# Another order for the ending of a convolution, GELU and rational-function kernel

## The chip, the cores and the metric

The kernel runs on one core of one Trainium2 chip. The metric is device time in microseconds of one execution, the median of several runs.

## The reference, cut to what matters

```python
# x: (2, 4096, 192); weight: (8, 7); w_in: (192, 2048); w_out: (2048, 192), two of each
w = softmax(weight)                       # per head, over the 7 taps
x = causal_depthwise_conv(x, w)           # 24 channels to a head
h = x.reshape(8192, 192) @ w_in1
g = h * sigmoid(1.702 * h)
x2 = g @ w_out1
h = x2 @ w_in2
P = a[0] + a[1] * h + a[2] * h**2 + a[3] * h**3
Q = 1 + abs(b[0]) * abs(h) + abs(b[1]) * h**2
out = (P / (Q + 1e-6)) @ w_out2           # (8192, 192)
```

## The kernel before, in words

The 8192 tokens are worked in 16 tiles of 512 (`NB = 16`, tiles 0 to 15). The 2048 hidden features are 16 blocks of 128, taken in 8 units of two blocks (`NS = 8`). The code writes the order of all engines by hand; each engine runs its own instructions in the order in which the program issues them.

For a tile n, the first layer is `h_product(0, n, i)` for unit i, then GELU on ACT, a split of the result into two float16 halves (`g1_high` on POOL, `g1_low` on DVE, into tiles `hl`), and the first output product `o1_main` and `o1_side`, which sums x2 of the whole tile in one PSUM tile `po` of the pool `ps_o`. x2 is scaled by a power of two: `x2_red` (DVE, maximum over the columns), `all_max` (a small TensorE product that spreads it over the partitions), `scales` (DVE), and `x2_split`, which writes x2's upper half (`high`, ACT) and lower half (`low`, DVE).

The second layer is `h_product(1, n, i)` ("product i" below; it needs both halves of x2), 24 matmuls into one PSUM tile `ph`. `unit` reads it: an absolute value and a linear step on ACT (L535, L536), two numerator steps on DVE (L537, L538). `denominator` (DVE, L543) makes Q; `log` and `inverse` (ACT, Ln and Sigmoid, L549 and L553, each kind in need of its own function table) turn it into 1/Q; `quotient` (DVE, L557) makes P/Q. `o2_chunk(n, i, k)` is the second output product of one block, 8 matmuls (L446) into another tile `po`; a pair of chunks (k = 0, 1) belongs to a unit.

PSUM has a pool `ps_h` of three buffers of two banks, for the `ph` tiles and small ones, and `ps_o` of one buffer of two banks.

The tiles overlap: the front phase of step j makes the first layer of tile j + 1 and the second layer of tile j; the back phase makes the first output product of tile j + 1, the logarithms and inverses of tile j, and the x2 scaling of tile j + 1. Output chunks of tile j that aren't done yet stand in a list `late_pe` and are issued between the products of the next step. `late_step` issues the quotients of units 4 to 7 of the tile before.

In the last step there is no later tile. The back phase then copies x2 from PSUM to SBUF (ACT, L691) before the scaling, since `po` of `ps_o` is needed for the output of tile 14. Four chunks of tile 14 are issued in the back phase, the other twelve in `last_phase`, which makes the products of tile 15 and its quotients, stores tile 14, and does all chunks of tile 15 at the end. The rows and names use the running numbers of the code: tile 14 is `NB - 2` and tile 15 is `NB - 1`.

Of the kernel before, what the change touches and what calls it, by code (L numbers as in the profile page):

```python
# [8 lines left out]
F32 = mybir.dt.float32  # L9
F16 = mybir.dt.float16  # L10
# [5 lines left out]
P = 128  # L16
# [4 lines left out]
def kernel(  # L21
# [30 lines left out]
    p2 = ctx.enter_context(tc.tile_pool(name="p2", bufs=2))  # L52
    p1 = ctx.enter_context(tc.tile_pool(name="p1", bufs=1))
    tiny = ctx.enter_context(tc.tile_pool(name="tiny", bufs=3))
    ps_h = ctx.enter_context(tc.tile_pool(name="ps_h", bufs=3, space=bass.MemoryType.PSUM))
    ps_o = ctx.enter_context(tc.tile_pool(name="ps_o", bufs=1, space=bass.MemoryType.PSUM))

    stack = ExitStack()
    stage = stack.enter_context(tc.tile_pool(name="stage", bufs=2))
    rings = []  # L60
# [11 lines left out]
    cst = const.tile([P, 8], F32, name="cst")  # L72

    def ps_tile(name):
        return ps_h.tile([P, 2, 512], F32, tag="h", name=name)

    def pow2_of(dst, src):
        nc.vector.tensor_scalar(out=dst, in0=src, scalar1=1e-30, scalar2=None, op0=ALU.max)
# [4 lines left out]
    def all_max(red, pm):  # L83

        nc.tensor.matmul(out=pm[:, 0, 0:P], lhsT=red.to_broadcast([P, P]), rhs=ident, start=True, stop=True)  # L85
# [217 lines left out]
    def flat_of(t):  # L303
        return t.rearrange("p k t -> p (k t)")[:, 0:W]
# [108 lines left out]
    def h_product(m, n, i, between=None):  # L413
        ph = ps_tile("ph")
        at = (ph, m, n, i)
        if m:
            h_side(*at, start=True)
            h_main(*at, stop=True)
        else:
            h_main(*at, start=True)  # L420
            if between is not None:
                between()
            h_side(*at, stop=True)
        return ph
# [53 lines left out]
    def o2_chunk(n, i, k, groups=range(NG)):  # L478
        pp = units_t[n][i][0]
        o_chunk(1, n, NS * k + i, ((pp, k, wo2[:, NS * k + i]),), groups)  # L480
# [47 lines left out]
    def unit(n, ph, pp=None):  # L528

        sc = sc2_t[n]  # L530
        if pp is None:
            pp = rings[0].tile([P, 2 * T], F32, tag="p", name="pp")
        qq = rings[0].tile([P, 2 * T], F32, tag="q", name="qq")
        h = ph.rearrange("p k t -> p (k t)")
        nc.scalar.activation(out=qq, in_=h, func=ACTF.Abs, scale=sc[:, 2:3])  # L535
        nc.scalar.activation(out=pp, in_=h, func=ACTF.Identity, scale=sc[:, 7:8], bias=sc[:, 6:7])  # L536
        nc.vector.tensor_tensor(out=pp, in0=pp, in1=h, op=ALU.mult)  # L537
        nc.vector.scalar_tensor_tensor(out=pp, in0=pp, scalar=sc[:, 5:6], in1=h, op0=ALU.add, op1=ALU.mult)  # L538
        units_t.setdefault(n, []).append((pp, qq))

    def denominator(n, i):
        qq = units_t[n][i][1]
        nc.vector.scalar_tensor_tensor(  # L543
            out=qq, in0=qq, scalar=ab[:, 14:15], in1=qq, op0=ALU.add, op1=ALU.mult
        )
# [5 lines left out]
    def inverse(n, i):  # L551
        qq = units_t[n][i][1]
        nc.scalar.activation(out=qq, in_=qq, func=ACTF.Sigmoid, scale=-1.0)  # L553

    def quotient(n, i):
        pp, qq = units_t[n][i]
        nc.vector.scalar_tensor_tensor(  # L557
            out=pp, in0=pp, scalar=ab[:, 0:1], in1=qq, op0=ALU.add, op1=ALU.mult
        )

    def each(f, n, steps):
        for i in steps:
            f(n, i)

    def late_step(n, i):

        if i < NS // 2:
            quotient(n, NS // 2 + i)
# [4 lines left out]
    def store(n):  # L573
        t = p1.tile([P, NG, D], F32, tag="on", name="on")
        for k in range(2):
            nc.scalar.activation(
                out=t[:, 2 * k:2 * k + 2], in_=out_tile(n, k), func=ACTF.Copy
            )
        po_t.pop((1, n)), sc2_t.pop(n)
        nc.sync.dma_start(out=out[n * T:(n + 1) * T].rearrange("(g p) d -> p g d", p=P), in_=t)  # L580
# [3 lines left out]
    def store_half(n, k):  # L584

        if k == 0:
            on_t[n] = p1.tile([P, NG, D], F32, tag="on", name="on")
        t = on_t[n][:, 2 * k:2 * k + 2]
        if k:
            nc.vector.tensor_copy(out=t, in_=out_tile(n, k))  # L590
        else:
            nc.scalar.activation(out=t, in_=out_tile(n, k), func=ACTF.Copy)
        rows = out[n * T + k * 2 * P:n * T + (k + 1) * 2 * P]
        nc.sync.dma_start(out=rows.rearrange("(g p) d -> p g d", p=P), in_=t)

    late_pe, early, second = [], {}, {}

    def last_phase(j):

        def units(i, late=0):  # L600
            pp = hl_tile().rearrange("p two t -> p (two t)").bitcast(F32)
            unit(j, h_product(1, j, i), pp)
            late_step(j - 1, i)
            for _ in range(late):
                late_pe.pop(0)()
            denominator(j, i)

        def own(i, groups=range(NG)):
            for k in range(2):
                o2_chunk(j, i, k, groups)  # L610

        first = NS // 2
        for i, late in enumerate((0, 0, 2, 1, 2, 2)):
            units(i, late)
        each(log, j, range(first))
        units(first + 2, 1)
        each(inverse, j, range(first))
        each(quotient, j, range(first - 1))
        units(first + 3, len(late_pe))
        quotient(j, first - 1)  # L620
        po_t[1, j] = ps_tile("po")
        for i in range(first):
            own(i)
        store(j - 1)
        each(log, j, range(first, NS))
        for i in range(first, NS):
            inverse(j, i)
            quotient(j, i)
        for i in range(first, NS - 1):
            own(i)  # L630
        for groups in (range(0, 2), range(2, 4)):
            own(NS - 1, groups)
        store_half(j, 0)
        store_half(j, 1)

    def front_phase(j, n1, extras):

# [30 lines left out]
    def back_phase(j, n1, n2, conv, splits):  # L668

        if conv is not None:  # L670
            x_transpose(conv)
            for k in range(K):
                x_conv_pool(conv, k)
        for part in (o1_main, o1_side):
            for i in range(NS):
                o1_product(part, n1, i, splits[i])
                if part is o1_main:
                    log(j, i)
            if part is o1_main and conv is not None:
                x_max(conv)  # L680
                x_scales(conv)
                x_scale_out(conv)
        chunks = [lambda i=i, k=k: o2_chunk(j, i, k) for i in range(NS) for k in range(2)]
        each(inverse, j, (0, 1, 2, 3))
        quotient(j, 0)
        src = po_t.pop((0, n1))
        pm = ps_tile("pm2")
        sc = sc2_t[n1] = tiny.tile([P, 24], F32, tag="sc2", name="sc2")
        if n2 is None:
            copy = p1.tile([P, 2, T], F32, tag="xc", name="copy")  # L690
            nc.scalar.activation(out=flat_of(copy), in_=flat_of(src), func=ACTF.Copy)  # L691
            src = copy
        red = x2_red(src)
        if n2 is None:
            chunks.pop(0)()
            all_max(red, pm)
        else:
            early[n2, 0] = h_product(0, n2, 0, lambda: all_max(red, pm))
            early[n2, 1] = h_product(0, n2, 1)
        scales(pm, sc)  # L700
        x2_split(n1, src, sc, sc1_t.pop(n1)[:, 6:7])
        each(quotient, j, (1, 2, 3))
        each(inverse, j, (4, 5, 6, 7))
        if n2 is not None:
            second[n1, 0] = h_product(1, n1, 0)
        for f in chunks[:3]:
            f()
        late_pe.extend(chunks[3:])
# [138 lines left out]
    with tc.manual_schedule():  # L847
        for j in range(NB - 1):
            n1, n2, conv = (j + d if j + d < NB else None for d in (1, 2, 3))
            extras = {i: [] for i in range(NS)}  # L850
            if conv is not None:
                x_load(conv)
                extras[2].append(lambda: x_red(conv))
            if j == 0:
                xc_t[2] = ps_o.tile([P, 2, 512], F32, tag="o", name="pc")
                for m in range(2 * K):
                    extras[m // 3].append(lambda m=m: x_conv_matmul(2, m))
                extras[5].append(lambda: x_high(2))
                extras[5].append(lambda: x_low(2))
            else:  # L860
                extras[NS - 2].append(lambda: store(j - 1))
                if n2 is not None:
                    extras[3].append(lambda: x_high(n2))
                    extras[4].append(lambda: x_low(n2))
            splits = front_phase(j, n1, extras)
            back_phase(j, n1, n2, conv, splits)
        last_phase(NB - 1)


# [25 lines left out]
```

## Time and profile before

| | |
|---|---|
| median of 3 runs | 1239.14 us (1234.54, 1239.14, 1240.14) |
| profiled execution | span 1239.7 us, first to last instruction; the page gives no other time for it |
| PE, DVE, ACT, POOL busy | 97%, 83%, 67%, 44% of the span |
| last matmul ends | 1235.7 us |
| granted TensorE clock, mean | 0.994 of full |

All times in the rows are microseconds from the start of the span unless marked ns. PE is TensorE, ACT ScalarE, DVE VectorE, POOL GpSimd. A line such as L446 is a line of the kernel before; a helper's line stands for all its calls. [...]

### The profile page before, as it was taken

Reading aid. Unit: us, or ns where it says so; the run is one execution under the profiler, and the core shown is the slowest. Engines: PE = TensorE matmul, PEld = TensorE weight load, DVE = VectorE, ACT = ScalarE, POOL = GpSimd, SP = SyncE. Lnnn points to the kernel's source line nnn. Section 1 sums busy time; section 2 is a strip of 40 time slices with the busy share of each in tenths; the row PEclk is TensorE's granted clock in tenths of the full one; section 3 lists DMA queues with packets and bytes.
Section 4 is the critical chain, followed back from the end, with each engine's and each line's share of the span. In section 5 each row is a group of like instructions: output and inputs, shape, how many; then the busy total and the mean of one; then the engine's idle time right before and its main releaser. Section 6 shows DMA issues by size and latency. Waiting matters only on the chain.

```text
span 1239.7 us, 24487 instructions
## 1 busy us (share of the span) xinstructions
PE 1200.2 (97%) x10762; PEld 957.8 (77%) x10762; DVE 1024.6 (83%) x1060; ACT 832.7 (67%) x832; POOL 545.4 (44%) x400
## 2 busy tenths in 40 slices
PE   4899999999999999999999999999999999999897
PEld 2537788787878888787878878787887878788587
DVE  4877989697988979798997979799696979868585
ACT  2724866849576685958667595866759486675775
POOL 3013563828355374735537382653738265213000
PEclk9999999999999999999999999999999999999899
DMA  7710001001010100101010010100001000000000
GB/s 214 228 51 14 1 1 27 1 1 28 1 27 1 27 2 1 27 1 27 1 27 2 2 27 1 28 1 27 1 2 27 1 14 2 14 1 14 1 1 26
DMA packets 32946, 27.87 MB, mean 22 GB/s; under 512 B 10485, under 2 KB 32073, under 8 KB 32073
## 3 DMA queue, kind: packets, MB, share of 16 engines
q1 hardware_dynamic: 32248, 26.31, 7.5%
q8 instruction: 84, 1.38, 0.5%
q14 instruction: 21, 0.17, 0.0%
q10 hardware_dynamic: 593, 0.01, 0.0%
HBM read 18.97 MB, written 6.29 MB: 20 GB/s over the span
## 4 chain that ended last, share of the span: by engine, by line
PE 84%; DVE 7%; ACT 6%; DMA 1%; issue 1%; ACTq 0%; DVEq 0%
PE ph L395 26%; PE po L446 25%; PE ph L408 13%; PE po L457 11%; PE po L467 6%; ACT qq L549 3%; PE pc L311 1%; DVE sc L338 1%; DMA wt<-in_weight_dram 1%; DVE xs L331 1%; DVE v L167 1%; PE pm L85 1%; ACT qq L553 1%; PE pt L265 1%; DVE v L176 1%
## 5 line engine op out<-in xcount | busy, mean ns | idle before, releaser
L495 POOL TENSOR_SCALAR hl<-g,sc 128x1024 f16<-128x1024 f32 x120 | 208.4, 1737 | 466.8 <-ACT g L485 466.8
L395 PE MATMUL ph<-xs,wm 128*128 128x256 f16 x3072 | 380.2, 274 | 3.0 <-ACT xs L328 2.2
L395 PEld LDWEIGHTS <-wm 128*128 128x128 f16 x3072 | 287.7, 98 | 74.8 <-issue 37.9
L446 PE MATMUL po<-wo,pp 128*128 128x192 f32 x1920 | 332.6, 328 | 5.9 <-ACT copy L691 3.0
L446 PEld LDWEIGHTS po<-wo,pp 128*128 128x128 f32 x1920 | 311.9, 191 | 7.6 <-ACT copy L691 3.2
L485 ACT ACTIVATE g<-ph,sc 128x1024 f32<-128x1024 f32 x120 | 133.9, 1116 | 176.1 <-PE ph L408 176.0
L535 ACT ACTIVATE qq<-ph,sc 128x1024 f32<-128x1024 f32 x128 | 142.6, 1114 | 141.1 <-PE ph L395 94.5
L557 DVE SCALAR_TENSOR_TENSOR pp<-pp,ab,qq 128x1024 f32<-128x1024 f32 x120 | 179.7, 1516 | 51.4 <-ACT qq L553 51.4
L408 PE MATMUL ph<-xs,wr 64*128 64x256 f16 x3072 | 196.4, 270 | 2.8 <-DVE xs L331 2.0
L543 DVE SCALAR_TENSOR_TENSOR qq<-qq,ab 128x1024 f32<-128x1024 f32 x128 | 197.3, 1541 | 0.0
L537 DVE TENSOR_TENSOR pp<-pp,ph 128x1024 f32<-128x1024 f32 x120 | 145.5, 1213 | 50.0 <-ACT pp L536 49.9
L408 PEld LDWEIGHTS <-wr 64*128 64x128 f16 x3072 | 138.2, 94 | 50.2 <-issue 33.2
L501 DVE SCALAR_TENSOR_TENSOR hl<-g,sc,hl 128x1024 f16<-128x1024 f32 x120 | 176.9, 1474 | 0.0
L325 POOL TENSOR_TENSOR xc<-xc,tap 128x768 f32<-128x768 f32 x78 | 162.8, 2087 | 6.5
L457 PE MATMUL po<-hl,wo 128*128 128x512 f16 x720 | 157.8, 379 | 0.0
L538 DVE SCALAR_TENSOR_TENSOR pp<-pp,sc,ph 128x1024 f32<-128x1024 f32 x120 | 153.7, 1281 | 4.3
L549 ACT ACTIVATE qq<-qq,eps,ab 128x1024 f32<-128x1024 f32 x128 | 146.9, 1230 | 0.2
L536 ACT ACTIVATE pp<-ph,sc 128x1024 f32<-128x1024 f32 x120 | 143.8, 1199 | 0.0
L321 POOL TENSOR_SCALAR tap<-xt,wt 128x512 f32<-128x512 f32 (+1 forms) x156 | 139.5, 906 | 6.4
L457 PEld LDWEIGHTS <-wo 128*128 128x128 f16 x720 | 70.4, 98 | 81.6
L553 ACT ACTIVATE qq<-qq 128x1024 f32<-128x1024 f32 x128 | 124.6, 1046 | 0.2
L467 PE MATMUL po<-hl,wo 128*64 128x256 f16 x1440 | 81.5, 273 | 0.0
(98 smaller groups left out, 694.0 us busy)
## 6 DMA issues: line engine op xcount, KB each, us to landing
raw<-in_moe_w_out_dram SPq DMA_DIRECT2D x8, 768.0 KB
out_dram<-on SPq DMA_DIRECT2D x15, 384.0 KB
xn<-in_x_dram SPq DMA_DIRECT2D x16, 256.0 KB
raw<-in_moe_w_in_dram SPq DMA_DIRECT2D x4, 1024.0 KB
xn<-in_x_dram SPq DMA_DIRECT2D x32, 64.0 KB
raw<-in_moe_w_in_dram SPq DMA_DIRECT2D x4, 512.0 KB
wr<-wr SPq DMA_DIRECT2D x8, 128.0 KB
out_dram<-on SPq DMA_DIRECT2D x2, 192.0 KB
```

The costliest lines, as they stand in the source:

```text
L325: nc.gpsimd.tensor_tensor(out=flat_of(c), in0=flat_of(c), in1=flat_of(d), op=ALU.add)
L395: nc.tensor.matmul(out=ph[:, h, k * TH:(k + 1) * TH], lhsT=wm[m][:, a_, f], rhs=xs[:, b_, h * TH:(h + 1) * TH], start=(start and k == 0 an ...
L408: nc.tensor.matmul(out=ph[:, h, k * TH:(k + 1) * TH], lhsT=wr[m][rows, a_, other, f], rhs=xs[rows, b_, T:W], start=(start and other == 0 a ...
L446: nc.tensor.matmul(out=dst, lhsT=tokens(t, k, g // 2)[:, g % 2 * P:(g % 2 + 1) * P], rhs=rhs, start=(done == 0 and g % 2 == 0 and q == 0), ...
L457: nc.tensor.matmul(out=po_t[0, n][:, 0].rearrange("p (h t) -> p h t", h=2), lhsT=w[:, 0:P], rhs=all_tokens(t, k), start=(at == 1 and q == ...
L467: nc.tensor.matmul(out=po_t[0, n][h * D2:(h + 1) * D2, 1, 0:TH], lhsT=w[:, P:D], rhs=tokens(t, k, h), start=(at == 1 and q == 0), stop=(at ...
L495: nc.gpsimd.tensor_scalar(out=hl[:, 0], in0=g, scalar1=sc1_t[n][:, 4:5], scalar2=1.0, op0=ALU.mult, op1=ALU.mult)
L501: nc.vector.scalar_tensor_tensor(out=hl[:, 1], in0=g, scalar=sc1_t[n][:, 4:5], in1=hl[:, 0], op0=ALU.mult, op1=ALU.subtract)
L538: nc.vector.scalar_tensor_tensor(out=pp, in0=pp, scalar=sc[:, 5:6], in1=h, op0=ALU.add, op1=ALU.mult)
L543: nc.vector.scalar_tensor_tensor(out=qq, in0=qq, scalar=ab[:, 14:15], in1=qq, op0=ALU.add, op1=ALU.mult)
L549: nc.scalar.activation(out=qq, in_=qq, func=ACTF.Ln, scale=ab[:, 15:16], bias=eps)
L557: nc.vector.scalar_tensor_tensor(out=pp, in0=pp, scalar=ab[:, 0:1], in1=qq, op0=ALU.add, op1=ALU.mult)
```

## The change

In the last step, `ending` takes the place of the back phase and of `last_phase`. x2 of the last tile is read in PSUM by `x2_red`, `high` and `low`, and isn't copied. The pool `ps_h` is closed after the last first-layer output product; its six banks become `ps_last`, one buffer of two banks for the output of tile 14, and `ps_two`, two buffers of two banks for `ph`. Quotient 1 of tile 14 is issued ahead of the lower half, and two pairs of its chunks before product 0. Products 0 and 1 are issued back to back. Then, for each unit i, come its readers, quotient i + 2 and the pair of chunks i + 2 of tile 14, an inverse, product i + 2, and the denominator of unit i, which is now two instructions on POOL. The logarithms of tile 15 are issued in groups of 4, 2 and 2 (4 and 4 before), and so are the inverses. All chunks of tile 15 come at the end, as before.

```diff
-    ps_h = ctx.enter_context(tc.tile_pool(name="ps_h", bufs=3, space=bass.MemoryType.PSUM))
     ps_o = ctx.enter_context(tc.tile_pool(name="ps_o", bufs=1, space=bass.MemoryType.PSUM))
 
+    ps_stack = ExitStack()
+    ps_hs = [ps_stack.enter_context(tc.tile_pool(name="ps_h", bufs=3, space=bass.MemoryType.PSUM))]
...
     def ps_tile(name):
-        return ps_h.tile([P, 2, 512], F32, tag="h", name=name)
+        return ps_hs[-1].tile([P, 2, 512], F32, tag="h", name=name)
...
-    def last_phase(j):
...
+    def pool_denominator(n, i):
+        qq = units_t[n][i][1]
+        t = flat2_of(p1.tile([P, 2, T], F32, tag="tap", name="sum"))
+        nc.gpsimd.tensor_scalar(
+            out=t, in0=qq, scalar1=ab[:, 14:15], scalar2=0.0, op0=ALU.add, op1=ALU.add
+        )
+        nc.gpsimd.tensor_tensor(out=qq, in0=qq, in1=t, op=ALU.mult)
...
+    def ending(j, splits):
+
+        n = j + 1
+        for part in (o1_main, o1_side):
+            for i in range(NS):
+                o1_product(part, n, i, splits[i])
+                if part is o1_main:
+                    log(j, i)
+        ps_stack.close()
+        po_t[1, j] = ctx.enter_context(tc.tile_pool(name="ps_last", bufs=1, space=bass.MemoryType.PSUM)).tile(
+            [P, 2, 512], F32, tag="l", name="po"
+        )
+        ps_hs.append(ctx.enter_context(tc.tile_pool(name="ps_two", bufs=2, space=bass.MemoryType.PSUM)))
+        src = po_t.pop((0, n))
+        each(inverse, j, (0, 1))
+        quotient(j, 0)
+        o2_chunk(j, 0, 0)
+        pm = ps_tile("pm2")
+        red = x2_red(src)
+        all_max(red, pm)
+        o2_chunk(j, 0, 1)
+        sc = sc2_t[n] = tiny.tile([P, 24], F32, tag="sc2", name="sc2")
+        scales(pm, sc)
+        xs = xs_t[1, n] = p2.tile([P, 2, W], F16, tag="xs2", name="xs2")
+        high(src, sc[:, 1:2], xs)
+        quotient(j, 1)
+        low(src, sc[:, 1:2], xs)
+        x2_scales(sc, sc1_t.pop(n)[:, 6:7])
+        each(inverse, j, (2, 3))
+        phs = {}
+
+        def product(i):
+            phs[i] = h_product(1, n, i)
+
+        def readers(i):
             pp = hl_tile().rearrange("p two t -> p (two t)").bitcast(F32)
-            unit(j, h_product(1, j, i), pp)
-            late_step(j - 1, i)
-            for _ in range(late):
-                late_pe.pop(0)()
-            denominator(j, i)
-
-        def own(i, groups=range(NG)):
+            unit(n, phs.pop(i), pp)
+
+        def own(m, i, groups=range(NG)):
             for k in range(2):
-                o2_chunk(j, i, k, groups)
+                o2_chunk(m, i, k, groups)
 
         first = NS // 2
...
+        own(j, 1)
+        product(0)
+        product(1)
+        for i in range(NS):
+            readers(i)
+            if i + 2 < NS:
+                quotient(j, i + 2)
+                own(j, i + 2)
+                if i + 4 < NS:
+                    inverse(j, i + 4)
+                product(i + 2)
+            pool_denominator(n, i)
+            if i == first:
+                each(log, n, range(first))
+            if i == first + 1:
+                each(inverse, n, range(first))
+            if i > first + 1:
+                quotient(n, i - first - 2)
+        store(j)
+        each(quotient, n, (2, 3))
+        for part in (range(first, NS - 2), range(NS - 2, NS)):
+            each(log, n, part)
+            for i in part:
+                inverse(n, i)
+                quotient(n, i)
+        for i in range(NS - 1):
+            own(n, i)
         for groups in (range(0, 2), range(2, 4)):
-            own(NS - 1, groups)
-        store_half(j, 0)
-        store_half(j, 1)
+            own(n, NS - 1, groups)
+        store_half(n, 0)
+        store_half(n, 1)
...
-        if n2 is None:
-            copy = p1.tile([P, 2, T], F32, tag="xc", name="copy")
-            nc.scalar.activation(out=flat_of(copy), in_=flat_of(src), func=ACTF.Copy)
-            src = copy
         red = x2_red(src)
...
-            back_phase(j, n1, n2, conv, splits)
-        last_phase(NB - 1)
+            if n2 is None:
+                ending(j, splits)
+            else:
+                back_phase(j, n1, n2, conv, splits)
```

## Rows read from the trace of the kernel before

**Rows 1.** The page, engine totals: busy us, share of the span, instructions.
```profile
PE 1200.2 (97%) x10762; PEld 957.8 (77%) x10762; DVE 1024.6 (83%) x1060; ACT 832.7 (67%) x832; POOL 545.4 (44%) x400
```
**Rows 2.** Busy time in three stretches: length, PE, PEld, DVE, ACT, POOL, clock, DMA.
```profile
1162.60:1179.50 16.90, 11.03 (x60) 9.56 (x62) 7.79 (x14) 7.62 (x9) 0.00 (x0) 0.80 0.00 0
1179.50:1206.00 26.50, 25.75 (x234) 21.68 (x235) 24.04 (x20) 19.97 (x18) 0.00 (x0) 1.00 0.00 1
1206.00:1235.70 29.70, 26.48 (x160) 25.62 (x159) 19.35 (x16) 20.39 (x21) 0.00 (x0) 1.00 0.04 14
```
**Rows 3.** Chain of waits, previous and last x2 scaling: start, us, what.
```profile
1092.52 0.88 DVE red L507
...
1164.81 0.70 ACT copy L691
...
1165.55 1.57 PE po L446 x8
1167.12 0.23 PE pm L85 x2
...
1168.33 0.94 ACT xs L328
...
1170.32 1.21 DVE pp L557
...
1171.57 5.49 PE po L446 x16
```
**Rows 4.** Timeline, products of the last tile: start, us, engine, line, form, wait.
```profile
1179.43 0.83 PE L408 MATMUL ph<-xs,wr 64*128 64x256 f16 x12
...
1179.54 1.11 ACT L535 ACTIVATE qq<-ph,sc 128x1024 f32<-128x1024 f32 x1 [6.49 <-PE ph L395]
...
1181.61 0.83 PE L408 MATMUL ph<-xs,wr 64*128 64x256 f16 x12
...
1183.69 2.77 PE L446 MATMUL po<-wo,pp 128*128 128x192 f32 x16
...
1184.23 1.28 DVE L557 SCALAR_TENSOR_TENSOR pp<-pp,ab,qq 128x1024 f32<-128x1024 f32 x1
...
1186.39 0.83 PE L408 MATMUL ph<-xs,wr 64*128 64x256 f16 x12
...
1204.49 1.48 PE L395 MATMUL ph<-xs,wm 128*128 128x256 f16 x12
```
**Rows 5.** Stretches around two pauses; first PE alone, then all engines, clock follows.
```profile
1168.50:1171.57 3.07, 0.15 (x2) 0.87 0.00 0
1171.57:1174.00 2.43, 2.43 (x8) 0.50 0.00 0
...
1211.20:1213.50 2.30, 0.01 (x1) 0.04 (x1) 2.30 (x3) 2.30 (x4) 0.00 (x0) 1.00 0.00 0
```
**Rows 6.** Timeline of DVE, first quotient of tile 14.
```profile
1162.00 1.28 DVE L557 SCALAR_TENSOR_TENSOR pp<-pp,ab,qq 128x1024 f32<-128x1024 f32 x1 [7.73 <-ACT qq L553]
```
**Rows 7.** Timeline of ACT and of PE, near the end.
```profile
1215.33 1.28 ACT L549 ACT_TABLE_LOAD   x1
1216.62 4.64 ACT L549 ACTIVATE qq<-qq,eps,ab 128x1024 f32<-128x1024 f32 x4
...
1225.01 10.67 PE L446 MATMUL po<-wo,hl 128*128 128x192 f32 x64 [0.88 <-DVE hl L557]
```
**Rows 8.** Timeline of POOL and DVE, two places in an earlier tile.
```profile
162.35 1.82 POOL L325 TENSOR_TENSOR xc<-xc,tap 128x768 f32<-128x768 f32 x1
162.40 2.85 DVE L557 SCALAR_TENSOR_TENSOR pp<-pp,ab,qq 128x1024 f32<-128x1024 f32 x1
...
169.76 1.22 DVE L537 TENSOR_TENSOR pp<-pp,ph 128x1024 f32<-128x1024 f32 x1 [1.46 <-ACT pp L536]
169.95 1.12 POOL L495 TENSOR_SCALAR hl<-g,sc 128x1024 f16<-128x1024 f32 x1
```
**Rows 9.** Groups by line on POOL, whole span: busy us, mean ns, idle before.
```profile
L495 POOL TENSOR_SCALAR hl<-g,sc 128x1024 f16<-128x1024 f32 x120 | 208.4, 1737 | 466.8 <-ACT g L485 466.8
```

More of the change, by code (lines that the diff above doesn't have):

```diff
@@ L596 @@
     late_pe, early, second = [], {}, {}
-    def last_phase(j):
-        def units(i, late=0):
-            pp = hl_tile().rearrange("p two t -> p (two t)").bitcast(F32)
-            unit(j, h_product(1, j, i), pp)
-            late_step(j - 1, i)
-            for _ in range(late):
-                late_pe.pop(0)()
-            denominator(j, i)
-        def own(i, groups=range(NG)):
+    def pool_denominator(n, i):
[5 more added lines that the diff above has]
+        nc.gpsimd.tensor_tensor(out=qq, in0=qq, in1=t, op=ALU.mult)
@@ new lines, in flat2_of @@
+    def flat2_of(t):
+        return t.rearrange("p k t -> p (k t)")
+    def ending(j, splits):
[30 more added lines that the diff above has]
+        def readers(i):
+            pp = hl_tile().rearrange("p two t -> p (two t)").bitcast(F32)
+            unit(n, phs.pop(i), pp)
+        def own(m, i, groups=range(NG)):
@@ L609, in own @@
             for k in range(2):
-                o2_chunk(j, i, k, groups)
+                o2_chunk(m, i, k, groups)
         first = NS // 2
[L613 to L630, printed above, removed]
+        own(j, 1)
[16 more added lines that the diff above has]
+                quotient(n, i - first - 2)
@@ L688, in back_phase @@
         sc = sc2_t[n1] = tiny.tile([P, 24], F32, tag="sc2", name="sc2")
-        if n2 is None:
-            copy = p1.tile([P, 2, T], F32, tag="xc", name="copy")
-            nc.scalar.activation(out=flat_of(copy), in_=flat_of(src), func=ACTF.Copy)
-            src = copy
         red = x2_red(src)
[L694 to L699, printed above, removed]
+        early[n2, 0] = h_product(0, n2, 0, lambda: all_max(red, pm))
+        early[n2, 1] = h_product(0, n2, 1)
         scales(pm, sc)
@@ L703, in back_phase @@
         each(inverse, j, (4, 5, 6, 7))
-        if n2 is not None:
-            second[n1, 0] = h_product(1, n1, 0)
+        second[n1, 0] = h_product(1, n1, 0)
         for f in chunks[:3]:
```

## The prediction

> **What bounds the kernel now.** I read the page's engine totals first. TensorE is busy for almost the whole span [rows 1], so the end moves only with the time in which PE stands still or runs at half clock, and with nothing else. All edits act after the last x1 output product of the last tile, which ends at 1162.6; what is before it stays as it is. Next I read the busy time of the stretches behind that point [rows 2]: PE is busy for 11.0 of 16.9 us while the last x2 is scaled, for 25.8 of 26.5 us in the last eight products, and for 26.5 of 29.7 us from there to its last matmul. Its pauses are 5.9 + 0.7 + 3.2 = 9.8 us.
>
> The chain of waits tells what the first pauses are [rows 3]: the inverses, the copy of x2 (0.70 us of the chain), the chunk that waited for the copy, the maximum, the scaling, x2's two halves, and then quotient 1, which stands behind the lower half on DVE. Sixteen matmuls then take 5.49 us. The same sixteen take 2.77 us in the loop [rows 4], and start to start 2.60. [...] That costs a further 3.0 us (2.9 here, and a little of the first product). The pause of 2.3 us at 1211.2 [rows 5] cost none: the clock is 1.00 from 1206 on [rows 2].
>
> PE's work in matmuls doesn't change: o1 products, 16 output chunks of tile 14, 8 products and 16 chunks of tile 15 stand on both sides. So the forecast is a list of the pauses after, against 9.8 + 3.0 = 12.8 us.
>
> **The x2 stage: copy gone, quotient 1 ahead of the lower half.** Before, quotient 0 is done at 1163.28 [rows 6], and chunk (0, 0) waits until 1165.55 for the copy. After, that chunk writes the new pool and starts at 1163.3. It takes 1.57 [rows 3], to 1164.9. The reduction reads PSUM instead of the copy; I price it like the 0.88 us of the stage before, in which x2 is read in PSUM [rows 3]: done at 1164.1, hidden by the chunk. The maximum starts at 1164.9. From its start to x2's upper half it is 1167.12 to 1168.33, or 1.2 us [rows 3]: 1166.1. Quotient 1 takes DVE from there to 1167.4, with the lower half behind it, 1168.4. PE does chunk (0, 1) until 1166.4, waits, does tile 14's second pair of chunks from 1167.4 to 1170.0, then product 0 to 1172.2. Before, product 0 ended at about 1179.5, where its reader starts [rows 4]. Gain 7.3 us; pauses of 0.7 and 0.9 instead of 3.0 and 2.9, and no clock loss here.
>
> **The loop: chunks between products, two PSUM buffers.** Product 1 follows to 1174.4. Now each pair of chunks needs a quotient that DVE issues behind the two numerator steps of the unit two places before. From the end of a product: its readers' absolute value at 1179.54 and quotient at 1184.23 are 4.7 us apart [rows 4]; the quotient 1.28 and a step 0.05; two chunks 2.60; the product 2.18 (1179.43 to 1181.61). Sum 10.8 us from product i to product i + 2. PE's own work for two places is 2 x (2.60 + 2.18) = 9.6. So the loop is bound by this latency, not by PE. Before, the chunks' quotients were ready and the products ran on.
>
> In numbers: product 0 ends at 1172.2, quotient 2 at 1178.2. PE pauses from 1174.4 to 1178.3, 3.9 us. Product 2 ends at 1183.0, product 4 at 1193.9. The odd ones lie between, product 3 at 1187.9, 5 at 1198.7, with pauses of 1.3 each before the even chunks. Behind unit 4's readers ACT has a table load and four logarithms, 1.28 + 4.64 = 5.9 us [rows 7], until 1202.0; unit 5's readers, due at 1198.8, are 3.2 us late. What is queued behind them is the rest: numerators, quotient 7 (done 1207.9), its chunks, and product 7, which ends at 1212.8. PE pauses 3.1 us before those chunks. Before, product 7 ended at 1206.0 [rows 4], with four chunks (5.2 us) still to do.
>
> **The tail.** Behind product 7 come its readers and numerators, 4.7 us, to 1217.5, then quotient 1 of tile 15. Before it PE has only unit 0's two chunks, so it pauses 2.4 and 1.9 us. From quotient 1 on (done 1219.7, below) everything is ready in time: quotients 2 to 5 follow in DVE's order; the two short rounds of logarithm and inverse add two table loads of 1.28 each, but quotient 7 is done at 1231 and its chunks come at 1235.4. So those loads hide behind PE; without that cover they would cost 2.6. Seven pairs of chunks at 2.60: 1219.7 + 18.3 = 1238.0. Before, the last matmul ended at 1235.7 [rows 7], and what follows it (the two copies and the last stores) is unchanged. The store of tile 14 now stands behind unit 7's readers on ACT, at about 1215, as before; on SP's queue only the last stores are behind it. So **+2.4 us**. Crosscheck by pauses: 0.7 + 0.9 + 3.9 + 1.3 + 1.3 + 3.1 + 2.4 + 1.9 = 15.5 against 12.8.
>
> **Denominators on POOL.** Eight DVE instructions of the quotient's form (1.28 us [rows 4]) go; POOL gets a one-input and a two-input pass per unit. The one-input pass of 1024 columns takes 1.12 [rows 8]. The two-input pass is shown only at 768 columns, 1.82 [rows 8]. I take 2.3 for 1024 (bounds 1.8, as for 768, and 2.9, with a DVE instruction ahead). The pair takes 3.4 us; it is wanted only by logarithms that come later, and POOL has nothing else to do here. But POOL and DVE exclude each other: a quotient that started 0.05 us behind a POOL product took 2.85 instead of 1.28 [rows 8]. A numerator step, which has one operand in PSUM, ran 1.22 beside POOL [rows 8], as usual. So only quotients collide. In the loop the pair of unit i ends 1.1 (absolute value) + 3.4 = 4.5 us behind its product, and the quotient is due at 4.7: just free. For unit 7, quotient 0 holds POOL up to 1215.0; its pair ends at 1218.4, and quotient 1 waits 0.9 us, which is in the 1219.7 above. Bounds for the pass of 1.8 and 2.9 give -0.5 and +1.1 at the end.
>
> Left on DVE, the denominators of units 6 and 7 would stand ahead of quotients 0 and 1 of tile 15: 2.4 us more of DVE work without POOL's 0.9 us of waiting, so quotient 1 some 1.5 later and the end near 1239.5. That is all that the move is worth by the rows. [...]
>
> **The clock.** Pauses of 3.9, 3.1, and 2.4 with 1.9 us are to come. Before, pauses of 3.0 and 2.9 together cost 3.0 us of speed, one of 2.3 cost nothing. Each of the long ones may cost up to 3.0 on the path, since the chunks behind it are on the chain: 0 to 6 for the two. I take one, 3.0. [...]
>
> Sum: 1239.7 + 2.4 + 3.0 = 1245.1 for the profiled execution. The median of the runs shown is 0.6 lower than that span, so **1244.5 us**, 0.4% slower; from 1241.5 (no clock loss) to 1247.5 (two).
>
> **Rivals.** *The loop runs at PE's pace, faster.* If the quotients were ready, six places of 4.8 us behind product 1 (1174.4) give product 7 at 1203.1; plus the 25.3 us of the tail, PE ends at 1228.4, and the time is 1231.9. For it: DVE is relieved of a quarter of its loop work. Against it: the 4.7 us of the readers are latency, not load. It decides if the step from product i to i + 2 is under 9.6. Chance 0.10.
>
> *Clock lost at each long pause, slower.* Two losses of 3.0, or a third in the tail: 1239.1 + 2.4 + 6 or 9 = 1247.5 to 1250.5. For it: the stretch from 1204 to 1220 has 7.4 us of pauses. Against: 2.3 us alone cost nothing. Chance 0.24.
>
> *POOL holds up the loop's quotients.* There is 0.2 us of room. If a pair takes 1 us more (POOL's one-input passes average 1.74 over the whole kernel, 0.6 over the free one [rows 9]), each of the four chained quotients starts 0.8 later: 3.2 more, 1247.7. Chance 0.08.
>
> *The copy was no loss:* if the x2 stage kept its old end, 7.3 us more, 1251.8. The stage before, without copy, speaks against it. Chance 0.02.
>
> My forecast keeps 0.56. Half a per cent, 6.2 us, is what a measurement of this kernel can tell from no change: 1232.9 to 1245.3. Of the forecast's share some 0.08 lies above that, so **faster 0.10, same 0.48, slower 0.42** (0.08 + 0.24 + 0.08 + 0.02). To leave out no more than 2 in 10, the range is 1237 to 1250.
>
> **What would show it.** Right: no copy on ACT; product 0 some 7 us earlier; product ends about 10.8 us apart two by two; a PE pause near 4 us behind product 1; readers of unit 5 behind the logarithms; about 18.3 us of chunks without a gap at the end. Wrong: chunks of the loop that start right behind products (first rival), a granted clock of 0.50 in two stretches (second), quotients of over 2 us in the loop (third).

## The result and the profile after

| | kernel before | changed kernel |
|---|---|---|
| median of 8 runs | 1237.38 us (1234.54 to 1240.14) | 1244.87 us (1239.41 to 1247.47) |
| ratio | | 1.0052, 95% interval 1.0036 to 1.0068 |
| second set | 1238.35 us (20 runs) | 1248.03 us (6 runs), ratio 1.0073 (1.0053 to 1.0093) |
| profiled execution, span | 1239.7 us | 1241.0 us (its own time 1242.78) |

The change makes the kernel slower by about a half per cent. 1244.5 was forecast, in a range of 1237 to 1250. The two spans can't be set against each other as they stand: the last first-layer output product ended at 1162.6 before, and ends at 1158.7 in the profiled execution of the changed kernel, though no instruction ahead of it was moved. The profiled execution of the kernel before was a long one: its span of 1239.7 is longer than that of every run of this kernel in the later sets (1232.3 to 1238.9). From the end of that product on all is compared.

The busy time of the changed kernel, cut at the end of the last first-layer output product, of product 0, of product 7 and of the last matmul. Columns: length, then PE, PEld, DVE, ACT, POOL busy, clock, DMA share, GB/s.

```profile
1158.72:1168.50 9.78, 8.10 (x60) 7.03 (x62) 5.23 (x12) 3.11 (x4) 0.00 (x0) 1.00 0.00 0
1168.50:1211.71 43.21, 33.60 (x265) 28.21 (x264) 24.46 (x20) 30.01 (x28) 40.54 (x13) 0.96 0.00 1
1211.71:1236.95 25.24, 21.34 (x129) 20.75 (x128) 15.97 (x11) 16.86 (x16) 11.06 (x4) 1.00 0.05 16
```

Before, the same three stretches took 16.9, 26.5 and 29.7 us [rows 2]: 73.1 together, against 78.2. The x2 stage is 7.1 us shorter, the tail 4.5 shorter, and the products 16.7 longer, so the ending is 5.1 us longer in these two profiles. Part of this is work that moved: four chunks of tile 14, 5.1 us of PE's time, stood behind product 7 before and stand ahead of it now. Without them the tail isn't shorter, and the products are 11.6 us longer. PE is idle for 1.7 + 9.6 + 3.9 = 15.2 us in the three stretches, where it was 9.8 before.

The chain of waits of the changed kernel, through the x2 stage, the first step of the loop, and the last (start, us, what):

```profile
1162.21 1.21 DVE pp L558
...
1163.46 2.87 PE po L447 x16
...
1168.59 1.11 ACT qq L536
1169.70 1.11 ACT hl L537
...
1170.83 1.23 DVE hl L538
...
1173.29 1.29 DVE pp L558
...
1174.62 4.55 PE po L447 x16
...
1196.12 4.63 ACT qq L550 x4
...
1216.53 1.90 DVE hl L558
...
1218.48 18.48 PE po L447 x112
```

Each step of the loop that was forecast is there: readers, numerators and the quotient of the chunk (L558) in one chain, so that the first pair of chunks of the loop starts at 1174.62, 6.1 us behind product 0's end; four logarithms on ACT in the path of unit 5's readers; then one unbroken stretch of 112 matmuls. The forecast had 18.3 us for that stretch. The first pair of chunks took 4.55 instead of 2.87 (the pair at 1163.46, also after a pause): PE had stood still for 3.9 us, and the granted clock was down. The pause and the chunks behind it, in the columns of the stretches above:

```profile
1170.60:1174.60 4.00, 0.08 (x1) 0.00 (x0) 3.73 (x4) 4.00 (x5) 3.92 (x2) 1.00 0.00 0
1174.60:1179.10 4.50, 4.48 (x16) 4.26 (x18) 4.44 (x3) 0.19 (x1) 4.40 (x2) 0.62 0.00 2
```

0.62 is the mean of a part at 0.50 of full (1175.0 to 1178.0) and one at 1.00 (from 1178.5 on); the loss is 38% of 4.5 us, 1.7 us.

One duration is far from the forecast. The groups on POOL, from 1165 to the end (busy us, mean ns, idle before):

```profile
L602 POOL TENSOR_SCALAR sum<-qq,ab 128x1024 f32<-128x1024 f32 x8 | 29.6, 3703 | 27.5 <-ACT qq L536 26.9
L605 POOL TENSOR_TENSOR qq<-qq,sum 128x1024 f32<-128x1024 f32 x8 | 22.0, 2747 | 0.7
```

The one-input pass takes 3.70 us where 1.12 was forecast, so POOL is busy nearly without a pause from the first unit to the last. Whether that sets the time was the first thing to test.

### The profile page after: what moved, and what is told of

The parts are those of the page before. It is cut to its first block, busy times and chain, and to the rows that moved or that the text cites. A ratio compares the mean times of both kernels' runs of the same rounds, so it can differ in the third digit from the quotient of the medians.

```text
span 1241.0 us, 24513 instructions
## 1 busy us (share of the span) xinstructions
PE 1197.3 (96%) x10762; PEld 956.7 (77%) x10762; DVE 1027.9 (83%) x1052; ACT 834.4 (67%) x833; POOL 594.4 (48%) x416
## 4 chain that ended last, share of the span: by engine, by line
PE 84%; DVE 8%; ACT 5%; DMA 1%; issue 1%; ACTq 0%; DVEq 0%
PE po L447 26%; PE ph L396 25%; PE ph L409 12%; PE po L458 11%; PE po L468 6%; ACT qq L550 3%; PE pc L312 1%; DVE sc L339 1%; DMA wt<-in_weight_dram 1%; DVE xs L332 1%; DVE v L168 1%; DVE pp L558 1%; PE pm L86 1%; PE pt L266 1%; DVE v L177 1%
## 5 line engine op out<-in xcount | busy, mean ns | idle before, releaser
L558 DVE SCALAR_TENSOR_TENSOR pp<-pp,ab,qq 128x1024 f32<-128x1024 f32 x120 | 178.8, 1508 | 51.2 <-ACT qq L554 51.2
L458 PEld LDWEIGHTS <-wo 128*128 128x128 f16 x720 | 70.5, 98 | 81.6
```

The source lines that it names most:

```text
L458: nc.tensor.matmul(out=po_t[0, n][:, 0].rearrange("p (h t) -> p h t", h=2), lhsT=w[:, 0:P], rhs=all_tokens(t, k), start=(at == 1 and q == ...
L558: nc.vector.scalar_tensor_tensor(out=pp, in0=pp, scalar=ab[:, 0:1], in1=qq, op0=ALU.add, op1=ALU.mult)
```

## The experiments

Theory A is that of the prediction: the loop waits for the latency of quotients that stand behind the numerators, and POOL is beside the path. Theory B: POOL's passes hold up the ending. Theory C: two PSUM buffers for the products instead of three do.

**The changed kernel again**, beside the next three.

> The changed kernel as it is, once more, as the base for the runs beside it. Both theories: 0.3 to 0.7% over the kernel before (1.0036 to 1.0068 was measured). In its profile, product 0 to product 7 about 43 us, with one stretch at half clock.

1248.03 us, ratio 1.0073 (1.0053 to 1.0093). Its stretches, in the same columns as above:

```profile
1160.60:1170.38 9.78, 8.11 (x60) 7.03 (x62) 5.22 (x12) 3.11 (x4) 0.00 (x0) 1.00 0.00 0
1170.38:1215.99 45.61, 36.00 (x264) 30.44 (x264) 25.95 (x21) 30.00 (x28) 42.35 (x14) 0.89 0.00 1
1215.99:1242.21 26.22, 23.01 (x128) 22.42 (x128) 13.78 (x10) 16.86 (x16) 9.24 (x3) 0.93 0.05 16
```

The same kernel, and 3.4 us more from the same place to the last matmul, with mean clocks of 0.89 and 0.93 instead of 0.96 and 1.00. PE's timeline shows where:

```profile
1176.50 5.46 PE L447 MATMUL po<-wo,pp 128*128 128x192 f32 x16 [3.94 <-DVE pp L558]
1209.45 4.36 PE L447 MATMUL po<-wo,pp 128*128 128x192 f32 x16 [3.00 <-DVE pp L558]
1222.06 20.15 PE L447 MATMUL po<-wo,hl 128*128 128x192 f32 x112 [2.44 <-DVE hl L558]
```

The same three in the first profile:

```profile
1174.62 4.55 PE L447 MATMUL po<-wo,pp 128*128 128x192 f32 x16 [3.94 <-DVE pp L558]
1206.67 2.87 PE L447 MATMUL po<-wo,pp 128*128 128x192 f32 x16 [3.00 <-DVE pp L558]
1218.48 18.47 PE L447 MATMUL po<-wo,hl 128*128 128x192 f32 x112 [1.64 <-DVE hl L558]
```

Against 2.87, 2.87 and 18.47 us, the loss is 5.8 us here and 1.7 there. One stretch at half clock was expected; here the clock is down in three, in parts with means of 0.75 (1170.38 to 1184.13), 0.95 (to 1215.99) and 0.93 (to 1242.21). So the clock behind the pauses differed between these two executions of one program, and cost 1.7 us in one and 5.8 in the other.

**Denominators back on DVE.**

```diff
-            pool_denominator(n, i)
+            denominator(n, i)
```

> Denominators back on DVE, nothing else. Theory A (the loop waits for the latency of quotients that stand behind the numerators; POOL is beside the path): within 2 us of the changed kernel, by the arithmetic of its own rows +2 (quotients 0 and 1 of the last tile stand behind two denominators). Theory B (POOL's slow passes, 3.70 and 2.36 to 3.2 us a unit, hold up the ending): 5 us or more faster than the changed kernel.

1248.32 us, ratio 1.0081 (1.0066 to 1.0097), not to be told from the changed kernel beside it. The stretch from product 0 to product 7, and the tail:

```profile
1169.92:1215.29 45.37, 35.82 (x264) 30.36 (x264) 32.09 (x27) 30.00 (x28) 0.00 (x0) 0.89 0.00 1
1215.29:1241.03 25.74, 22.80 (x129) 21.99 (x128) 14.15 (x12) 16.86 (x16) 0.00 (x0) 0.93 0.05 16
```

45.4 us with POOL idle, and 45.6 with POOL busy for 42 of them: POOL isn't what the loop waits for. The 2 us that the arithmetic gave for this undoing can't be seen either.

**POOL's pass with other operations.**

```diff
-            out=t, in0=qq, scalar1=ab[:, 14:15], scalar2=0.0, op0=ALU.add, op1=ALU.add
+            out=t, in0=qq, scalar1=ab[:, 14:15], scalar2=1.0, op0=ALU.mult, op1=ALU.mult
```

> POOL's one-input pass of the denominator with two multiplications instead of two additions, so that the denominators' values are other ones; shapes and places stay. If the kind of operation sets the 3.70 us: the pass takes about 1.1 us, and the time stays within 1.5 us of the changed kernel (theory A, POOL is beside the path) or falls by 3 us or more (theory B). If the width or the source sets it: 3.7 us again.

The pass writes other values, so the denominators are other ones; shapes and places stay. 1246.72 us, ratio 1.0068 (1.0052 to 1.0083). The groups on POOL:

```profile
L605 POOL TENSOR_TENSOR qq<-qq,sum 128x1024 f32<-128x1024 f32 x8 | 18.9, 2364 | 0.7
L602 POOL TENSOR_SCALAR sum<-qq,ab 128x1024 f32<-128x1024 f32 x8 | 9.9, 1240 | 45.4 <-ACT qq L536 44.1 <-DVE pp L558 1.2
```

The same shape took 1.24 us in the mean with two multiplications (1.12 was priced) and 3.70 with two additions. POOL's work fell from 51.6 to 28.8 us and the time stayed. Theory B is out for the changed kernel.

**Quotients ahead of the numerators.**

```diff
+            if i + 2 < NS:
+                quotient(j, i + 2)
             readers(i)
             if i + 2 < NS:
-                quotient(j, i + 2)
                 own(j, i + 2)
```

> Quotient i + 2 issued ahead of unit i's numerators instead of behind them, denominators stay on POOL. Theory A: chunks no longer wait, product 7 ends some 7 to 9 us earlier, the pause near 4 us behind product 1 and the half clock behind it go; then POOL becomes the late one (its pair takes 6.1 us a unit, PE's places 4.8) and the end gains only 3 to 5 us. Theory B: no gain. Theory C (two PSUM buffers instead of three are what slows the loop): no gain, product to product stays at 10.8 us for two places.

1243.08 us, ratio 1.0035 (1.0022 to 1.0048), 5 us under the changed kernel of the same set. Product 0 to product 7:

```profile
1170.19:1209.24 39.05, 32.89 (x265) 27.38 (x264) 22.90 (x17) 29.58 (x28) 36.76 (x12) 0.91 0.00 1
```

The pause behind product 1 is gone, and product 0 to product 7 takes 6.6 us less than in the changed kernel beside it. Part of what is left is now POOL's. ACT's timeline:

```profile
1190.53 3.50 ACT L550 ACTIVATE qq<-qq,eps,ab 128x1024 f32<-128x1024 f32 x3
1199.14 1.24 ACT L550 ACTIVATE qq<-qq,eps,ab 128x1024 f32<-128x1024 f32 x1 [5.10 <-POOL qq L605]
```

The fourth logarithm waits 5.1 us for POOL's denominator, and the readers of unit 5 stand behind it. Once PE no longer waits for quotients, POOL's long pass is on the path.

**Both.** The two edits above (the first and the third) together.

> Both: quotients ahead of the numerators and denominators on DVE. Theory A: 4 to 7 us faster than the changed kernel, product 0 to product 7 in some 32 to 34 us instead of 43. Theory B: the gain of the denominators on DVE alone. Theory C: no gain in the loop.

1238.52 us, ratio 1.0008 (0.9999 to 1.0018): 0.65% under the changed kernel of the same set by the two ratios, or 8 us, more than expected. Product 0 to 7, and the stretch behind it:

```profile
1168.58:1200.99 32.41, 31.49 (x265) 26.55 (x264) 27.81 (x23) 27.57 (x26) 0.00 (x0) 1.00 0.00 1
1200.99:1232.23 31.24, 23.79 (x129) 23.50 (x128) 16.96 (x14) 19.19 (x19) 0.00 (x0) 0.84 0.04 13
```

In the loop PE is busy 31.5 of 32.4 us with the same two buffers, so theory C is out. But the tail is 31.2 instead of 25 to 26 us: PE reaches the last tile's chunks 11 to 13 us earlier and finds no quotient. It stands still for 7.5 us, and the clock of the tail is 0.84 in the mean. Against the run with the denominators on DVE alone the loop gains 13.0 us, and 5.5 of them are given back in the tail (31.2 instead of 25.7).

**Four quotients early as well.**

```diff
             if i == first + 1:
                 each(inverse, n, range(first))
-            if i > first + 1:
-                quotient(n, i - first - 2)
+                each(quotient, n, range(first))
         store(j)
-        each(quotient, n, (2, 3))
```

> Quotients ahead, denominators on DVE, and the last tile's quotients 0 to 3 issued right behind their inverses, ahead of the last two units' numerators. Theory A: PE goes from product 7 straight into the last tile's chunks; by the arithmetic of rows 10 us faster than the changed kernel, about 1235 us, and some 5 to 7 us faster than the kernel before. Theory C (two PSUM buffers): no faster than the kernel before.

1232.95 us, ratio 0.9960 (0.9948 to 0.9972): faster than both kernels. The same two stretches:

```profile
1169.13:1201.54 32.41, 31.51 (x265) 26.53 (x264) 28.92 (x24) 27.57 (x26) 0.00 (x0) 1.00 0.00 1
1201.54:1226.73 25.19, 23.14 (x128) 22.40 (x128) 15.86 (x14) 19.18 (x19) 0.00 (x0) 0.93 0.05 16
```

The loop of 32.4 us stays and the tail is 25.2 again; from the last first-layer output product to the last matmul it is 67.4 us, against 73.1 before and 78.2 to 81.6 in the changed kernel.

**The store of tile 14 later**, on top of that.

```diff
-        store(j)
...
                 quotient(n, i)
+            if part[0] == first:
+                store(j)
```

> The version with quotients ahead, denominators on DVE and four early quotients, and the store of the tile before moved behind the logarithms and inverses of units 4 and 5. In the profile PE paused 1.9 us for quotient 4, and the two copies of the store stood 0.87 us ahead of that table load on ACT. Expected: the pause falls to about 1.0 us, 1 to 2 us faster than without the move (the more where the half clock behind the pause goes too). Rival (the store's place is hidden): within 0.5 us.

1234.45 us, ratio 0.9969 (0.9957 to 0.9980): no gain, a miss. PE's timeline:

```profile
1203.04 10.67 PE L447 MATMUL po<-wo,hl 128*128 128x192 f32 x64
1215.10 5.47 PE L447 MATMUL po<-wo,hl 128*128 128x192 f32 x32 [1.40 <-DVE hl L558]
1222.62 5.47 PE L447 MATMUL po<-wo,hl 128*128 128x192 f32 x32 [2.04 <-DVE hl L558]
```

The pause ahead of quotient 4's chunks fell from 1.9 to 1.4 us, and the lower clock behind it, 0.64 over 4.7 us, went: the clock is 1.00 over the whole tail. But the store now stands ahead of the last logarithms, and PE, which got there at full speed, pauses 2.0 us for quotient 6. The wait moved from one quotient to another: from the last first-layer output product to the last matmul it is 67.4 us, as without the move.

**The new x2 stage with the old loop.** The x2 stage and pools of the changed kernel; then quotients 2 and 3 at once, and products, chunks, denominators, logarithms and inverses in the order of the kernel before.

```diff
         own(j, 1)
+        each(quotient, j, (2, 3))
+        each(inverse, j, (4, 5, 6, 7))
...
+        def units(i, late=0):
+            product(i)
+            readers(i)
+            late_step(j, i)
+            for _ in range(late):
+                chunks.pop(0)()
+            denominator(n, i)
+
+        for i, late in enumerate((0, 2, 2, 1, 2, 2)):
+            units(i, late)
```

> The changed x2 stage and PSUM pools, with the loop and the tail in the order of the kernel before (quotients two units and more ahead, denominators on DVE, logarithms and inverses in two groups of four). Theory A: the x2 stage's 7 us remain, less what two PSUM buffers cost; by the arithmetic of rows 6 to 7 us faster than the changed kernel and 3 us faster than the kernel before, about 1234 us. Theory C: product 0 to product 7 stays near 40 us, and the time is no better than the kernel before.

1236.06 us, ratio 0.9986 (0.9976 to 0.9996): 1.7 us faster than the kernel before by the ratio, with an interval that leaves out 1, where 3 were expected. Product 0 to product 7, and the tail:

```profile
1168.84:1199.19 30.35, 28.64 (x250) 24.21 (x250) 26.52 (x22) 19.57 (x19) 0.00 (x0) 1.00 0.00 1
1199.19:1229.80 30.61, 26.33 (x145) 25.74 (x143) 17.03 (x14) 21.00 (x21) 0.00 (x0) 0.89 0.04 13
```

The x2 stage is 9.78 us long as in the changed kernel, so the ending takes 70.7 us against 73.1 before. Of the 7.1 us that the x2 stage gains, 4.7 are given back behind it: PE stands still for 4.3 us in the tail, and the clock falls (0.89). The x2 stage is the part of the change that gains.

**The copy of x2 put back**, ahead of the first two inverses.

```diff
+        copy = p1.tile([P, 2, T], F32, tag="xc", name="copy")
+        nc.scalar.activation(out=flat_of(copy), in_=flat_of(src), func=ACTF.Copy)
+        src = copy
         each(inverse, j, (0, 1))
```

> The changed kernel with the copy of x2 to SBUF put back, x2 scaled from the copy, own PSUM pools kept. Theory A (what gains in the x2 stage is the output's own bank and quotient 1 ahead of the lower half, so that PE never waits for the copy): 0 to 1 us slower than the changed kernel, product 0 ends within 1 us of where it was. Rival (the copy itself is the gain): product 0 ends 2 us or more later.

1251.09 us, ratio 1.0102 (1.0084 to 1.0120). Product 0 ends 5.2 us later, and the expectation of theory A fell. The chain of waits shows why:

```profile
1160.80 0.81 ACT copy L625
...
1161.63 1.28 ACT L554
...
1162.92 1.06 ACT qq L554
...
1164.02 1.29 DVE pp L558
```

On ACT the copy waits for x2's last matmul, and behind it stand the table load, the inverse and with it quotient 0, which otherwise are done, or under way, when that matmul ends. So the place was tested, not the copy.

**The copy behind the inverses.** The same three lines, one line further down.

> The copy of x2 put back once more, now behind the first two inverses on ACT. In the first try it stood ahead of them, and its wait for x2 held up the table load, the inverses and quotient 0 (product 0 ended 5.2 us later). Theory A, mended (the copy costs only what it delays; with the output in its own bank nothing on PE waits for it): product 0 ends within 0.5 us of where the changed kernel has it, 9.8 us behind the last first-layer output product, and the time is that of the changed kernel within 2 us. Rival (the copy itself was the loss): product 0 ends 2 us or more later.

1248.4 us, ratio 1.0075 (1.0061 to 1.0089), the changed kernel's time. The x2 stage:

```profile
1159.47:1169.25 9.78, 8.11 (x60) 7.04 (x62) 5.31 (x12) 3.84 (x5) 0.00 (x0) 1.00 0.00 0
```

9.78 us with the copy, 9.78 without: with tile 14's output in a bank of its own, the copy is hidden behind quotient 0 and its chunk.

**Quotient 1 behind the lower half**, as in the kernel before.

```diff
-        quotient(j, 1)
         low(src, sc[:, 1:2], xs)
         x2_scales(sc, sc1_t.pop(n)[:, 6:7])
+        quotient(j, 1)
```

> The changed kernel with quotient 1 behind the lower half and the scale factors on DVE, as in the kernel before, nothing else. Theory A (PE's second pair of chunks waits for quotient 1): product 0 ends 2 to 3 us later, the time is 2 to 5 us longer with the half clock that a longer pause may bring. Rival (the pair is hidden): product 0 where it was.

1252.45 us, ratio 1.0108 (1.0092 to 1.0123), 0.35% or 4 us over the changed kernel by the two ratios. Its x2 stage, by stretch and by chain:

```profile
1159.09:1174.57 15.48, 10.87 (x60) 9.52 (x62) 5.30 (x12) 3.10 (x4) 0.00 (x0) 0.78 0.00 0
```

```profile
1165.52 1.21 DVE pp L558
...
1166.77 5.49 PE po L447 x16
```

5.7 us longer, where 2 to 3 were expected: the quotient came 2.9 us later (6.4 us behind the start of the stretch instead of 3.5), and the 16 matmuls behind the longer pause took 5.49 us, as before the change [rows 3], instead of 2.87. So of the x2 stage's gain of 7.1 us, 5.7 come from the order of one DVE instruction, the clock behind the longer pause included. The remaining 1.4 would fit the output's own bank, or the two inverses fewer ahead of x2's scaling on ACT; neither was undone by itself, so which it is stays open.

## Why the prediction was right

**The x2 stage.** Forecast 7.3 us, measured 7.1. The pauses there were put at 0.7 and 0.9 us; both measure 0.84. The working named the copy's removal first; behind the inverses, with the output in its own bank, the copy costs nothing (9.78 us with it and without), and quotient 1's place gives most of the gain, clock included. So the sum was right and the share of the copy in it was not. The fourth rival was right that the copy was no loss, and wrong that the stage would then keep its old end.

**The loop.** The step from product i to i + 2 was put at 10.8 us, and the pause behind product 1 at 3.9, which it is (3.94, in the first profile and the second). In the changed kernel the third pair of chunks starts 12.8 us behind the first (1174.62 to 1187.46), which has the half clock in it, and the fifth 11.2 behind that (1198.62). That the latency of the quotient sets it is shown: with the denominators on DVE in both, the loop shrinks from 45.4 to 32.4 us when the quotients are issued ahead. Of these 13.0 us, 8.6 are PE's standing still (9.55 to 0.92) and 4.3 its busy time (35.82 to 31.49), with a mean clock of 0.89 in the one and 1.00 in the other. That the four logarithms hold unit 5's readers is in the chain above; the pause that follows was put at 3.1 us and takes 3.0. All pauses together were put at 15.5 us and came to 15.2.

**The tail.** Forecast 25.3 us from product 7 to the last matmul, measured 25.2 and 26.2. Quotient 1 took 1.90 us instead of 1.28 in the chain (1216.53), with a POOL pass that had started 0.2 to 0.3 us ahead of it: a hold-up of 0.6 us, where 0.9 was forecast.

**Denominators on POOL.** Here a term was mis-sized: the one-input pass was priced with a row of two multiplications, 1.12 us [rows 8], and took 3.70 with two additions. The two-input pass was put at 2.3 and takes 2.36 where nothing collides. The error cost nothing that can be seen, since this loop doesn't wait for POOL: 28.8 us of POOL work or 51.6 give the same time. That it cost nothing is luck, for the working left only 0.2 us of room. The third rival, POOL holding up the loop's quotients, had the pair 3 us longer where its condition asks for 1, and didn't come. Its sign, a quotient of over 2 us, showed once (2.15 us, at 1176.93), at quotient 3, whose chunks don't wait; the four that carry the chain took 1.28 each.

**The clock.** One loss of 3.0 us was taken, as behind the pauses of before, where the clock was 0.50 [rows 5]; 0 to 6 were the bounds. The first profile lost 1.7 us, the second 5.8. So the second rival, two losses or three, is no separate case but what the same kernel did in its second profile. What was forecast as one number is a spread. The clock doesn't explain all of it: the first profile has a mean granted clock of 0.997, the other thirteen runs of the two sets 0.992 or 0.993, and those thirteen take from 1239.41 to 1248.75 us. What sets the rest of the spread is open.

**The level.** The ending grew by 5.1 and 8.5 us in the two profiles, and the medians by 7.5 and 9.7; 5.4 was forecast from the profiled execution. That 1244.5 meets 1244.87 so closely is in part luck. The working started from a median of three runs, 1239.14, and set the time 0.6 us under the span; eight runs have 1237.38, and a run's time is 2.2 us over its own span for the kernel before (in every run of the later sets) and 1.8 over it for the changed kernel. So the start was 1.8 us too high and the growth 2.1 us too small, and the two errors cancel.

**The first rival**, a loop at PE's pace, comes about in another order, with the quotients ahead of the numerators: 32.4 us for the loop, and with four early quotients 1232.95 us, near the 1231.9 that was worked out for it.

## What to carry to other kernels

In a software pipeline, look at where an instruction stands in its engine's queue, not only at how busy the engine is: here one quotient ahead of the lower half was worth 4 us, and quotients behind the numerators made the loop 45.4 instead of 32.4 us (denominators on DVE in both), though DVE was busy for only 32 of the 45. Part of a gain ahead of a wait was given back where the next wait stayed (5.5 of 13.0 us, 4.7 of 7.1), so follow the freed engine to the place where it stops next. A pause of TensorE cost twice in some of these executions, by standing still and by the clock behind it (0.62 behind 3.94 us, 0.64 behind 1.91), and the second part differed from run to run: behind the same pause of 3.94 us, 16 matmuls took 4.55 us in one execution and 5.46 in another.

## What the runs showed of the hardware that was not expected

POOL's one-input pass over 128 x 1024 float32 took 3.70 us with two additions and 1.24 with two multiplications, in the same place (one of the constants was changed with them, from 0.0 to 1.0). And the pass of 3.70 us didn't keep DVE out for all of that time. The rows of the changed kernel on DVE and POOL:

```profile
1176.93 2.15 DVE L558 SCALAR_TENSOR_TENSOR pp<-pp,ab,qq 128x1024 f32<-128x1024 f32 x1
...
1186.13 1.28 DVE L558 SCALAR_TENSOR_TENSOR pp<-pp,ab,qq 128x1024 f32<-128x1024 f32 x1
...
1190.91 1.28 DVE L558 SCALAR_TENSOR_TENSOR pp<-pp,ab,qq 128x1024 f32<-128x1024 f32 x1
```

```profile
1176.89 3.71 POOL L602 TENSOR_SCALAR sum<-qq,ab 128x1024 f32<-128x1024 f32 x1
...
1183.13 3.70 POOL L602 TENSOR_SCALAR sum<-qq,ab 128x1024 f32<-128x1024 f32 x1
...
1189.73 3.70 POOL L602 TENSOR_SCALAR sum<-qq,ab 128x1024 f32<-128x1024 f32 x1
```

A quotient that started 0.04 us behind such a pass took 0.87 us longer; one that started 3.0 us into another took its usual 1.28, though the pass ran on for 0.7 us. A third, which started 1.2 us into a pass and lies wholly inside it, took 1.28 too. The prediction took it from one row that POOL and DVE exclude each other: 2.85 us instead of 1.28 for a quotient behind a two-input pass of 1.82 [rows 8]. For these two quotients of 1.28 us it doesn't hold. Why the pass with two additions took longer is open.
